# Sigmoid attention and routed rows on one core: scores and values interleaved by halves, routed work in one block a step

## The chip, the core and the metric

The kernel runs on one core of a Trainium2 chip. The metric is the device time of one execution in microseconds (us); lower is better. TensorE (PE) multiplies, VectorE (DVE) and ScalarE (ACT) work element-wise, GpSimd (POOL) and SyncE (SP) here mostly issue DMAs. Each engine works through its own list of instructions in order and waits at semaphores for the others.

## The reference

Two layers in fp32, one behind the other. The first is attention with a sigmoid in place of softmax; the second routes the best 128 tokens of each of the 8 sequences through a small MLP.

```python
# q, k, v: (8, 12, 448, 64)
scores = scale * q @ k^T - log(448)
x = (sigmoid(scores) @ v)            # then as (8, 448, 768)
# w_gate: (768,), w1: (768, 1024), w2: (1024, 768), capacity: 128
scores = einsum('bsd,d->bs', x, w_gate)
out = x.copy()
for b in range(8):
    top = argpartition(-scores[b], 128)[:128]
    xe = x[b, top]
    g = sigmoid(scores[b, top])
    out[b, top] = xe + g[:, None] * (maximum(xe @ w1, 0) @ w2)
```

## The kernel before

**Attention.** The 8 x 12 heads are taken as 24 quads of four heads; a step `s` (12 of them) takes two quads, and three quads make a batch. q and k are loaded token-major (`raw_q`, `raw_k`), turned on DVE in 32x32 blocks (`turn`, two buffers each), and the scores are computed transposed, so that keys lie on partitions. All attention matmuls are 32x64 tiles of weights on 448 columns: sixteen for one *unit* of scores (`unit`, L311; seven units a step), which fill two PSUM tiles `psc` of two heads each; ACT applies the sigmoid to each tile (L319, "squash" below) and puts it into SBUF. Values are computed by `values(s, n)` in four rounds a step (L359), each round accumulating into the two PSUM tiles `o0` (first quad) and `o1` (second). `values(s, 0)` follows unit 6 of its step, and rounds 1 to 3 follow units 0 to 2 of the next step. When the fourth round is done, `take` (L377) transposes each half of `o0` and `o1` on DVE into the batch's activations `x_b`, four takes a step; only then can the two PSUM tiles hold something else. PSUM is full: two `psc`, `o0`, `o1`, two banks each.

**Routing.** For each quad `gate_part` multiplies x_b with the gate weights and sums (L385, L388, two of each a quad). With a batch's third quad `gate` adds up the parts (L403 to L418) and issues a DMA of the 448 scores to DRAM on POOL (L413). `spread` then reads them back as a copy on all 128 partitions, `rep` (L425, POOL's queue too). `ranking` compares every score with the scores that a partition holds (L433, L436) and makes a one-hot matrix `hot` of the ranks (L446, L448; for batches 2 to 5 also two sums of it, L457 and L461). `choose` multiplies it on PE into the 128 chosen tokens (L472, L476), `fetch` turns that into indices and gathers these rows of `out`, which `store` has written.

**Routed work.** Two batches make a pair. Chosen rows are transposed on PE (`turn_rows`, L518). The two products with w1 and w2 are done in seven block products each, after Strassen's scheme: `first` (24 matmul records, L557) and `second` (8, L622), with sums of weight quarters that `make_sum` computes once on DVE, keeps in DRAM and `lend` loads into attention buffers that are free for a while. 28 first and 28 second products are made; the table `WORK` puts most of them behind units 3, 4 and 5 of steps 4 to 11, the rest into `rest()` behind the last step.

**Order.** The schedule is manual: the order of the program is the order of each engine. `gap(s, n)` follows each unit with values, items of `WORK`, gates and what `put` has registered: `spread(b)` after unit 4 of the step in which the batch is complete, `ranking(b)` after unit 1 of the step behind it (for batch 1, after the takes of that step), `choose` some units later in it. In steps 1 to 3, in which there is no routed work yet, `keep_busy` (L332) puts four matmuls of no use between units.

Of the kernel before, what the change touches and what calls it, by code (L numbers as in the profile page):

```python
# [17 lines left out]
def kernel(  # L18
# [11 lines left out]
    nc = tc.nc  # L30
# [31 lines left out]
    raw = ctx.enter_context(tc.tile_pool(name="raw", bufs=2))  # L62
    vals = ctx.enter_context(tc.tile_pool(name="vals", bufs=1))
    head = ctx.enter_context(tc.tile_pool(name="head", bufs=2))
# [6 lines left out]
    ps_sc = ctx.enter_context(tc.tile_pool(name="ps_sc", bufs=2, space=PSUM))  # L71
    ps_o = [ctx.enter_context(tc.tile_pool(name=f"ps_o{n}", bufs=1, space=PSUM))
            for n in range(2)]
    turns = [0, 0]

    def banks(which):
        if which == "any":
            turns[1] ^= 1
            which = "psc" if turns[1] else "o"
        if which == "psc":  # L80
            return ps_sc.tile([P, 2, 512], F32, name="psc")
        if which == "o":
            turns[0] ^= 1
            which = turns[0]
        return ps_o[which].tile([P, 2, 512], F32, name=f"o{which}")


    raws, raw_v = {}, {}

    def load(i):  # L90

        if i >= NQ:
            return
        if i == 2:
            both = moe.tile([P, 6 * KH * P], F32, name="rows_t")
            raws[i] = [both[:, n * TB * Dh:(n + 1) * TB * Dh] for n in range(2)]
        else:
            raws[i] = [raw.tile([P, TB * Dh], F32, name=f"raw_{nm}") for nm in "kq"]
        for t, src in zip(raws[i], (k, q)):
            nc.sync.dma_start(  # L100
                out=t, in_=bass.AP(tensor=src.tensor, offset=src.offset + i * 4 * S * Dh,
                                   ap=[[TB * Dh, P], [1, TB * Dh]]))

    def load_v(s):


        if s >= NS:
            return
        if s in (1, 3):
            tv = [moe.tile([P, D], F32, name="xe", bufs=3).rearrange("p (h c) -> p h c", h=4)  # L110
                  for _ in range(2)]
            at = 2 * QW + s // 2 * 4 * Dh
            th = room["all"][:, at:at + 4 * Dh].rearrange("p (h c) -> p h c", h=4)
        else:
            t = vals.tile([P, 8, NF * Dh], F32, name="raw_v")
            tv = [t[:, :4], t[:, 4:]]
            th = vals.tile([P, 4, Dh], F32, name="raw_h")
        raw_v[s] = (tv, th)

        def blocks(h, r, nh, n):  # L120
            return bass.AP(tensor=v.tensor,
                           offset=v.offset + (8 * s + h) * S * Dh + r * Dh,
                           ap=[[TB * Dh, TT], [S * Dh, nh], [1, n * Dh]])

        for m in range(4):
            rows = slice(m * TT, (m + 1) * TT)
            if s in (1, 3):
                for x in range(2):
                    nc.sync.dma_start(out=tv[x][rows], in_=blocks(4 * x, NF * m, 4, NF))
            else:  # L130
                nc.sync.dma_start(out=t[rows], in_=blocks(0, NF * m, 8, NF))
        for n in range(4):
            nc.sync.dma_start(out=th[n * TT:(n + 1) * TT],
                              in_=blocks(4 * (n // 2), HK + n % 2, 4, 1))


# [4 lines left out]
    assert D == 4 * NF * Dh and 2 * QW + 8 * Dh <= 7 * FH * P  # L141
# [26 lines left out]
    def load_left(m):  # L168

        if m == 1:  # L170
            t = moe.tile([P, 7 * FH * P], F32, name="hidden")
            room["all"], room["a"], room["b"] = t, t[:, :QW], t[:, QW:2 * QW]
        load_quarter(m, room["a"], (1, 0) if m == 1 else (0, 1))

    def make_sum(m, key):
        if (m, key) == (1, 6):
            room["c"] = moe.tile([P, 6 * KH * P], F32, name="rows_t")[:, :QW]
        a, b, c = [room.get(x) for x in "abc"]
        w00, wx, w11 = [(w1_sb, w2_sb)[m - 1][:, x] for x in range(3)]
        dst, x, y, op = {  # L180
            (1, 5): (b, a, w11, ALU.add), (1, 6): (c, b, w00, ALU.subtract),
            (1, 7): (a, w00, a, ALU.subtract), (1, 3): (b, wx, c, ALU.subtract),
            (2, 5): (b, a, w00, ALU.subtract), (2, 6): (c, w11, b, ALU.subtract),
            (2, 7): (a, a, w11, ALU.subtract), (2, 4): (b, wx, c, ALU.subtract)}[m, key]
# [5 lines left out]
    SUMS = {(1, 5): [(1, 5), (1, 6)], (1, 6): [(1, 7), (1, 3)],  # L190
            (2, 5): [(2, 5), (2, 6)], (3, 5): [(2, 7), (2, 4)]}

    def attn_tile(pr, slot):
        return attnp.tile([P, 2, S], F32, name=f"attn{pr}_{slot}")

    def lend(m, key, slot):


        halves = []
        for pr in range(2):  # L200
            if slot == "raw":
                t = raw.tile([P, TB * Dh], F32, name=f"raw_{'kq'[pr]}")[:, :QW // 2]
            elif slot == "turned":
                t = head.tile([P, 2, TB, TT], F32, name=f"{'kq'[pr]}T")
                t = t.rearrange("p e r t -> p (e r t)")[:, :QW // 2]
            else:
                t = attn_tile(pr, slot).rearrange("p a s -> p (a s)")[:, :QW // 2]
            nc.sync.dma_start(out=t, in_=sums[m, key][:, pr * QW // 2:(pr + 1) * QW // 2])
            halves.append(t)
        lent[m, key] = halves  # L210
# [58 lines left out]
    qT, kT, attn, outs = {}, {}, {}, {}  # L269

    def turn(i):


        if i >= NQ:
            return
        kT[i] = head.tile([P, 2, TB, TT], F32, name="kT")
        qT[i] = head.tile([P, 2, TB, TT], F32, name="qT")
        sk, sq = [t.rearrange("p (r e d) -> p e r d", e=2, d=TT) for t in raws.pop(i)]
        for e in range(2):
            nc.vector.transpose(kT[i][:, e, :HK],  # L280
                                sk[:, e, :HK].rearrange("p (m c) d -> p c m d", c=NF))
        nc.vector.transpose(kT[i][:, :, HK:], sk[:, :, HK:])
        if i == 0:
            for e in range(2):
                nc.vector.transpose(qT[i][:, e], sq[:, e])
        else:
            nc.vector.transpose(qT[i], sq)  # L287

    def two_blocks(s):


        return s > 5 and (s, 4) not in WORK

    def unit(s, n):


        if ((s == 0 and n in (1, 3, 5)) or (s in (1, 2, 3) and n == NF + 1)
                or (two_blocks(s) and n == NF + 2)):
            psc = [banks(0), banks(1)]
        else:  # L300
            psc = [banks("psc"), banks("psc")]
        if n == NF:
            parts = [(x, HK) for x in range(2)]
        else:
            x, c = divmod(n, NF + 1)
            parts = [(x, 4 * c), (x, 4 * c + 2)]
        for e in range(2):
            for y, (x, r) in enumerate(parts):
                for h in range(4):
                    d = slice(h * TT, (h + 1) * TT)  # L310
                    nc.tensor.matmul(  # L311
                        psc[h // 2][y * Dh:(y + 1) * Dh, h % 2, :S],
                        kT[2 * s + x][d, e, r:r + 2, :].rearrange("d r t -> d (r t)"),
                        qT[2 * s + x][d, e].rearrange("d r t -> d (r t)"),
                        start=(e == 0), stop=(e == 1))
        for pr in range(2):
            a = attn_tile(pr, f"d{s % 2}{n}" if n < 3 else f"u{n}")
            attn[s, pr, n] = a
            nc.scalar.activation(a, psc[pr][:, :, :S], AF.Sigmoid, bias=bias_s, scale=QK_SCALE)  # L319

    x_tiles, gate_parts, st = {}, {}, {}

    def open_outs(s):
        if s not in outs:
            outs[s] = [banks(0), banks(1)]

    def keep_busy(s):


        open_outs(s)  # L330
        for _ in range(4):
            nc.tensor.matmul(outs[s][0][:, 0, :HP * TT], iden,  # L332
                             wg_b.rearrange("p h t -> p (h t)"), start=True, stop=True)

    def values(s, n):

        tv, th = raw_v[s]  # L340
        if n == 0:
            open_outs(s)
        o = outs[s]
        first = (0, 2, 2, 0)[n]
        quads = [(first + m) % 4 for m in range(4)]
        work = [(r, c) for c in range(NF) for r in quads]
        if n < 2:
            at = 4 * (NF - 1)
            work[at:at] = [(r, None) for r in quads]
        for r, c in work:  # L350
            x, pr = divmod(r ^ n, 2)
            rows = slice(r * TT, (r + 1) * TT)
            for j in range(2):
# [12 lines left out]
        else:  # L366
            for x in range(2):
                for pr in range(2):
                    take(s, pr, x)
# [520 lines left out]
```

## Time and profile before

| what | value |
| --- | --- |
| three runs | 455.09, 455.43, 457.24 us, median 455.43 |
| the profiled execution | 455.12 us, its span 453.3 us |
| PE busy | 441.8 us (97%) |
| DVE, ACT busy | 303.8 us (67%), 180.9 us (40%) |
| mean granted TensorE clock | 0.998 |
| first unit of scores begins | 6.31 us |
| steps 1, 2, 3 (attention alone) | 24.8, 24.7, 25.8 us |
| steps 4 to 11 (with routed work) | 30.4, 35.2, 36.0, 31.8, 36.4, 36.0, 32.5, 30.6 us |
| the rest, behind step 11 | 86.4 us |

The profile records one execution; its span is the time between the first and the last instruction, and the execution's own time is 1.8 us more. Busy time of PE is the time in which a matmul ran, not time at full rate: a matmul that is held up, or records that overlap, count as busy too. Each matmul of fp32 leaves two records. A step is counted from the first record of its values, as a table of windows has it. The chain of waits follows the work that ended last backwards through its releasers.

### The profile page before, as it was taken

Reading aid. Unit: us, or ns where it says so; the run is one execution under the profiler, and the core shown is the slowest. Engines: PE = TensorE matmul, PEld = TensorE weight load, DVE = VectorE, ACT = ScalarE, POOL = GpSimd, SP = SyncE. Lnnn points to the kernel's source line nnn. Section 1 sums busy time; section 2 is a strip of 40 time slices with the busy share of each in tenths; the row PEclk is TensorE's granted clock in tenths of the full one; section 3 lists DMA queues with packets and bytes.
Section 4 is the critical chain, followed back from the end, with each engine's and each line's share of the span. In section 5 each row is a group of like instructions: output and inputs, shape, how many; then the busy total and the mean of one; then the engine's idle time right before and its main releaser. Section 6 shows DMA issues by size and latency. Waiting matters only on the chain.

```text
span 453.3 us, 14449 instructions
## 1 busy us (share of the span) xinstructions
PE 441.8 (97%) x6398; PEld 277.7 (61%) x6398; DVE 303.8 (67%) x663; ACT 180.9 (40%) x234; POOL 32.6 (7%) x55
## 2 busy tenths in 40 slices
PE   8999999999999999999999999999999999999994
PEld 3474745566744845666577854665555648769952
DVE  4308669993854897779633797797662849894472
ACT  3856464555545254335345445324434520101100
POOL 7000000010000000010010000010020001001001
PEclk9999999999999999999999999999999999999999
DMA  8798998999866985985665983995923999711001
GB/s 272 196 342 197 347 345 169 268 196 328 172 208 211 158 228 175 181 193 190 155 235 165 143 219 115 210 176 175 254 80 113 254 212 265 145 36 71 1 0 69
DMA packets 128334, 84.67 MB, mean 187 GB/s; under 512 B 97600, under 2 KB 112064, under 8 KB 128272
## 3 DMA queue, kind: packets, MB, share of 16 engines
q1 hardware_dynamic: 126288, 75.84, 64.9%
q0 software_dynamic: 1984, 7.91, 5.8%
q8 instruction: 50, 0.82, 0.8%
q14 instruction: 12, 0.10, 0.1%
HBM read 63.28 MB, written 20.46 MB: 185 GB/s over the span
## 4 chain that ended last, share of the span: by engine, by line
PE 83%; DVE 9%; DMA 4%; issue 2%; ACT 1%; POOLq 0%; SPq 0%; DVEq 0%
PE o L359 26%; PE psc L311 22%; PE o L557 12%; PE o L622 8%; PE psc L622 5%; PE psc L557 5%; PE o L311 4%; DVE x_b L377 3%; DMA scores<-total 2%; DVE scr L385 1%; DVE gate_p L388 1%; DMA raw_q<-in_q_dram 1%; DVE xe L633 1%; DMA rep<-scores 1%; DMA out_dram<-xe,idx 1%
## 5 line engine op out<-in xcount | busy, mean ns | idle before, releaser
L311 PE MATMUL psc<-qT,kT 32*64 32x448 f32 x2336 | 145.1, 540 | 1.5 <-ACT attn_u L319 0.9
L359 PE MATMUL o<-attn_d,raw_v 32*64 32x448 f32 x960 | 107.6, 535 | 0.1
L359 PE MATMUL o<-attn_u,raw_v 32*64 32x448 f32 x960 | 104.8, 535 | 0.3 <-issue 0.2
L319 ACT ACTIVATE attn_u<-psc,bias_s 128x896 f32<-128x896 f32 x76 | 72.5, 1005 | 76.7 <-PE psc L311 71.3
L311 PEld LDWEIGHTS psc<-qT,kT 32*64 32x64 f32 x2336 | 62.1, 131 | 53.6 <-issue 32.6
L319 ACT ACTIVATE attn_d<-psc,bias_s 128x896 f32<-128x896 f32 x70 | 66.8, 1005 | 46.8 <-PE psc L311 46.7
L377 DVE STREAM_TRANSPOSE x_b<-o 128x448 f32<-128x448 f32 x48 | 26.9, 617 | 63.1 <-PE o L359 55.6
L359 PEld LDWEIGHTS o<-attn_u,raw_v 32*64 32x64 f32 x960 | 44.0, 132 | 21.5 <-issue 17.8
L359 PEld LDWEIGHTS o<-attn_d,raw_v 32*64 32x64 f32 x960 | 43.1, 132 | 17.2 <-issue 14.4
L573 ACT ACTIVATE hidden<-hidden 128x512 f32<-128x512 f32 x12 | 7.5, 630 | 63.2 <-DVE hidden L570 63.2
L557 PEld LDWEIGHTS o<-rows_t,w_sb 128*128 128x128 f32 x264 | 30.3, 192 | 3.8 <-issue 1.4
L557 PE MATMUL o<-rows_t,w_sb 128*128 128x128 f32 x264 | 31.6, 277 | 0.4 <-DVE rows_t L524 0.3
L388 DVE TENSOR_REDUCE gate_p<-scr 128x14 f32<-128x448 f32 x48 | 29.8, 622 | 1.7
L385 DVE TENSOR_TENSOR scr<-x_b,wg_b 128x448 f32<-128x448 f32 x48 | 29.5, 616 | 1.0
L280 DVE STREAM_TRANSPOSE kT<-raw_k 128x384 f32<-128x384 f32 x46 | 23.5, 548 | 7.3 <-DMA raw_k<-in_k_dram 7.3
L433 DVE TENSOR_SCALAR_CACHE_REDUCE scr<-rep,who 128x448 f32<-128x448 f32 (+1 forms) x32 | 21.5, 672 | 9.9 <-DMA rep<-scores 9.1
L557 PEld LDWEIGHTS o<-rows_t,attn_d 128*128 128x128 f32 x216 | 24.7, 192 | 2.6 <-DVE xe L633 1.5
L557 PE MATMUL o<-rows_t,attn_d 128*128 128x128 f32 x216 | 25.7, 276 | 0.6 <-DVE rows_t L530 0.3
L622 PE MATMUL o<-w_sb,hidden 128*128 128x384 f32 x72 | 24.7, 490 | 0.2 <-PE psc L311 0.2
L287 DVE STREAM_TRANSPOSE qT<-raw_q 128x896 f32<-128x896 f32 x22 | 23.6, 1072 | 1.1 <-DMA raw_q<-in_q_dram 1.1
L359 PE MATMUL o<-attn_d,xe 32*64 32x448 f32 x192 | 24.1, 535 | 0.0
L570 DVE TENSOR_TENSOR hidden<-o,hidden 128x512 f32<-128x512 f32 x22 | 14.6, 686 | 13.7 <-PE o L557 13.5
(117 smaller groups left out, 517.9 us busy)
## 6 DMA issues: line engine op xcount, KB each, us to landing
attn_d<-sum SPq DMA_DIRECT2D x42, 384.0 KB, 5.8
out_dram<-x_b SPq DMA_DIRECT2D x32, 336.0 KB, 6.5
raw_k<-in_k_dram SPq DMA_DIRECT2D x23, 448.0 KB
raw_q<-in_q_dram SPq DMA_DIRECT2D x23, 448.0 KB, 6.8
raw_v<-in_v_dram SPq DMA_DIRECT2D x40, 192.0 KB, 8.3
w_sb<-in_moe_w_dram SPq DMA_DIRECT2D x6, 768.0 KB
sum<-hidden SPq DMA_DIRECT2D x6, 768.0 KB, 6.3
rep<-scores POOLq DMA_DIRECT2D x7, 224.0 KB, 5.6
```

The costliest lines, as they stand in the source:

```text
L280: nc.vector.transpose(kT[i][:, e, :HK], sk[:, e, :HK].rearrange("p (m c) d -> p c m d", c=NF))
L287: nc.vector.transpose(qT[i], sq)
L311: nc.tensor.matmul(psc[h // 2][y * Dh:(y + 1) * Dh, h % 2, :S], kT[2 * s + x][d, e, r:r + 2, :].rearrange("d r t -> d (r t)"), qT[2 * s + ...
L319: nc.scalar.activation(a, psc[pr][:, :, :S], AF.Sigmoid, bias=bias_s, scale=QK_SCALE)
L359: nc.tensor.matmul(o[x][j * Dh:(j + 1) * Dh, pr, :S], w, a[rows, j, :], start=(n == 0 and c == 0), stop=(n == 3 and c == NF - 1))
L377: nc.vector.transpose(x_tiles[b][:, :, 2 * g + pr, :], outs[s][x][:, pr, :S].rearrange("p (r t) -> p r t", t=TT))
L385: nc.vector.tensor_tensor(out=tmp, in0=x_tiles[b][:, :, hp, :], in1=wg_b[:, hp:hp + 1, :].to_broadcast([P, TB, TT]), op=ALU.mult)
L388: nc.vector.tensor_reduce(out=gate_parts[b][:, :, hp], in_=tmp, axis=AX.X, op=ALU.add)
L433: nc.vector.tensor_scalar(out=junk[:n], in0=rep[:n], scalar1=own, scalar2=0.0, op0=ALU.is_gt, op1=ALU.add, accum_out=above[:n, c:c + 1])
L557: nc.tensor.matmul(ps[:, f, :n], w((t * FH + f) * P, P), x[:, t, :n], start=(t == 0), stop=(t == KH - 1))
L570: nc.vector.tensor_tensor(out=dst, in0=a, in1=b, op=ALU.add)
L622: nc.tensor.matmul(ps[:n, :DH], h[:, t, :n], w(t * DH, DH), start=(t == 0), stop=(t == FH - 1))
```

## The change

PSUM is held in four tiles that keep their roles: `a1`, `a0` for scores (`PA`), `o1`, `o0` for values (`PO`). The order of one step is that of seven *slots*. A slot is two halves; a half holds four matmuls of scores on two row groups, eight of values on the other two row groups, four of scores again, and one squash. Values run at a distance of four slots: slots 0 to 3 hold rounds 3 to 6 of the step before, slots 4 to 6 rounds 0 to 2 of their own. A unit takes two key blocks of both quads (in `chunks` and `column`; the first four units of step 0 those of one quad). One slot of a step is split, the second part of its values coming ahead of the scores, with a small ACT copy (`join`) between its parts. The takes follow slot 3.

Routed work stands in one `block(s)` after slot 3 of steps 4 to 11, in the order of `BLOCKS`, its products going through the banks of the four tiles from `o0` on. Choices ("c") stand in the blocks too. In `block`, or behind slot 3 where there is none, q and k of the next step are turned; q is turned in place, raw k has one buffer, and the pool of turned q and k has four buffers each. Behind the block come `gates(2s-2)` and `gates(2s-1)`, the gates of both quads of the step before. `spread(b)` comes after slot 5 or 6 of that step, `ranking(b)` after slot 1 of the step behind it, for all batches (the steps of `FULL` are 2, 3, 5, 6, 8, 9, 11 and 12). The sums of the weights are made later (`SUMS`), and lent sums go to buffers of their own (`spares`) after slot 4. `keep_busy` is gone.

The main parts of the diff:

```diff
-    ps_sc = ctx.enter_context(tc.tile_pool(name="ps_sc", bufs=2, space=PSUM))
-    ps_o = [ctx.enter_context(tc.tile_pool(name=f"ps_o{n}", bufs=1, space=PSUM))
-            for n in range(2)]
+    tiles = {}
+    for name in ("a1", "a0", "o1", "o0"):
+        pool = ctx.enter_context(tc.tile_pool(name=f"ps_{name}", bufs=1, space=PSUM))
+        tiles[name] = pool.tile([P, 2, 512], F32, name=name)
+    PA, PO = [[tiles[f"{c}{n}"] for n in range(2)] for c in "ao"]
...
-    SUMS = {(1, 5): [(1, 5), (1, 6)], (1, 6): [(1, 7), (1, 3)],
-            (2, 5): [(2, 5), (2, 6)], (3, 5): [(2, 7), (2, 4)]}
+    SUMS = {(1, 4): [(1, 5)], (1, 6): [(1, 7)], (2, 1): [(1, 6)], (2, 4): [(1, 3)],
+            (4, 4): [(2, 5)], (4, 6): [(2, 7)], (5, 1): [(2, 6)], (5, 2): [(2, 4)]}
...
+            if which == "q":
+                if i:
+                    nc.vector.transpose(heads["q", i], heads["q", i])
...
+    def value(s, half, p, n):
+        for r in (2 * half, 2 * half + 1):
+            x, c, step = chunks(s, n, half)
+            pr = r % 2 ^ p
+            rows = slice(r * TT, (r + 1) * TT)
+            at = column(s, n, half) * Dh
+            i = done[s, x, pr] = done.get((s, x, pr), 0) + 1
+            for j in range(2):
+                nc.tensor.matmul(PO[x][j * Dh:(j + 1) * Dh, pr, :S],
+                                 raw_v[s][rows, 2 * pr + j, at:at + Dh],
+                                 attn[s, pr, n][rows, j, :],
+                                 start=((s, x, pr, j) not in done), stop=(i == TB))
+                done[s, x, pr, j] = True
...
+    BLOCKS = {
+        4: [("t", 0), (1, 0, 1), ("c", 1)],
+        5: [("t", 1), (1, 0, 2), (1, 0, 6)],
+        6: [(1, 0, 7), (1, 0, 4), (1, 0, 5), ("c", 2), (1, 0, 3), (2, 0, 1)],
+        7: [(2, 0, 2), (2, 0, 4), (2, 0, 3), (2, 0, 5), (2, 0, 6), ("c", 3), ("t", 2)],
+        8: [(2, 0, 7), ("t", 3), (1, 1, 1), (1, 1, 2), (1, 1, 6), (1, 1, 7), (1, 1, 4)],
+        9: [(1, 1, 5), (1, 1, 3), (2, 1, 1), ("c", 4), (2, 1, 2), (2, 1, 4)],
+        10: [(2, 1, 3), (2, 1, 5), (2, 1, 6), ("c", 5), (2, 1, 7), ("t", 4)],
+        11: [(1, 2, 1), ("t", 5), (1, 2, 2)],
+    }
...
+    def block(s):
+        places = [("o0", 0), ("o0", 1), ("a1", 0), ("a1", 1), ("a0", 0), ("a0", 1),
+                  ("o1", 0), ("o1", 1)]
+        at = 0
+        for i, item in enumerate(BLOCKS[s]):
...
+            if i == 1:
+                turn("q", 2 * s + 2)
+                turn("k", 2 * s + 3)
+                load("k", 2 * s + 4)
+            if i == 2:
+                turn("q", 2 * s + 3)
...
+    FULL = [(NG * b + NG - 1) // 2 + 1 for b in range(B)]
+    def rounds(s):
...
+        same = [(0, 0, 1), (1, 0, 1), (1, 2, 3), (0, 2, 3), (0, 4, 5)]
+        if s + 1 in BLOCKS:
+            return same + [(1, 4, 5), (1, 0, 6)]
+        return same + [(0, 1, 6), (1, 4, 5)]
...
+    def slot(s, n):
...
+        for half in range(2):
+            pr = 1 - half
+            a, b = entries(vs, i, half)
...
+                score(s, n, 0, pr, PA[pr])
+                value(vs, half, *a)
+                value(vs, half, *b)
+            score(s, n, 1, pr, PA[pr])
...
+            squash(s, n, pr, PA[pr])
+            if i == 6:
+                takes(vs, half)
...
+    def after(s, n):
+        if n == NF and s:
+            if 4 < s:
+                load_v(s)
+            if s in BLOCKS:
+                block(s)
+            else:
+                turn("q", 2 * s + 2)
+                turn("k", 2 * s + 3)
+                load("k", 2 * s + 4)
+                turn("q", 2 * s + 3)
+            gates(2 * s - 2)
+            gates(2 * s - 1)
+        if n == NF + 1:
+            for i, (m, key) in enumerate(LENT.get(s + 1, ())):
+                lend(m, key, i)
...
+        for key in SUMS.get((s, n), ()):
+            make_sum(*key)
...
+        for b in range(B - 1):
+            full = FULL[b]
+            if (s, n) == (full, 5 + b % 2):
+                spread(b)
+            if (s, n) == (full, 6):
+                store(b)
+            if (s, n) == (full + 1, 1):
+                ranking(b)
...
         for s in range(NS):
             for n in range(NU):
-                unit(s, n)
...
+                if n == 0 and s:
+                    load("q", 2 * s + 2, 2 * s + 3)
+                    turn("k", 2 * s + 2)
+                    load("k", 2 * s + 3)
+                slot(s, n)
+                after(s, n)
         rest()
```

## The prediction

> **What bounds the kernel now.** The page comes first: its shares of busy time and the chain that ended last.
>
> ```profile
> PE 441.8 (97%) x6398; PEld 277.7 (61%) x6398; DVE 303.8 (67%) x663; ACT 180.9 (40%) x234; POOL 32.6 (7%) x55
> PE 83%; DVE 9%; DMA 4%; issue 2%; ACT 1%; POOLq 0%; SPq 0%; DVEq 0%
> ```
>
> PE is busy 441.8 of 453.3 us, yet the chain leaves it for 17% of the span. So I ask what PE's records cost at full rate, and what the rest of the chain is. The chain of waits from 57 to 130 us (start, us, what; x counts records, and a matmul is two) answers both:
>
> ```profile
> 59.77 2.24 DVE x_b L377 x4
> ...
> 66.55 7.38 DMA scores<-total
> ...
> 74.50 3.54 DMA rep<-scores
> ...
> 78.07 0.70 DVE scr L433 x2
> ...
> 84.94 1.18 DVE x_b L377 x2
> 86.12 0.14 issue
> 86.26 1.04 PE o L476 x8
> ...
> 98.03 1.50 PE psc L311 x32
> 99.53 3.01 PE o L359 x64
> ```
>
> A unit of scores is 32 records in 1.50 us, two rounds of values 64 in 3.01, so small-tile work costs 0.376 us per 8 records. Further down, the first unit after a 128x128 product takes 1.69, and such a product between units 2.88 where a run of them shows 2.68 each: a change of tile size costs 0.19 each way. Upward is batch 0's routing: quads taken, gates, scores out on POOL at 66.55, copies landed at 78.07, ranking on DVE to 84.9, and then, behind it on the same engine, two takes (L377) for which PE waits.
>
> **Full rate.** The changed kernel has the same products, without keep_busy: 5,376 small records / 32 × 1.504 = 252.7; 28 first products × 2.68 = 75.0; 28 second × 2.58 = 72.2; 8 row turns × 0.66 = 5.3; choosing 5.4. Sum 410.6. With 6.3 us ahead of the first unit (6.31) and 6.0 behind the last matmul (447.3 to 453.3), 422.9. Before, whose span is 453.3, loses 30.4, of which keep_busy is 3 × 1.5.
>
> **Slots.** A slot is one unit of scores plus one round of values, 3.01 us, on other row groups in turn. A score tile's turn is 8 records of scores and 16 of values (3 × 0.376 = 1.13), the last record of its scores (0.53), the squash on ACT (1.00) and some 0.2 of handing over: 2.87, under the 3.01 of a slot, so ACT hides by 0.14. A step is 7 × 3.008 = 21.06; steps 1 to 3 of before took 24.8, 24.7 and 25.8. Losses that stay:
> - Step 0: four units alone need 8 squashes × 0.905 = 7.2 of ACT against 6.0 of PE, and the first squash (1.0) has no cover: 2.2.
> - Split slots of steps 1 to 3 free a score tile late: 3 × 0.5 = 1.5.
> - One block per step: 8 × 0.38, and 0.4 in the rest: 3.4.
> - Block 4's row turn, its copy (0.8) and product wait on each other: 1.0. In blocks 5, 8 and 11 the first item waits for a take of o0 (1.12 with a lag of 0.4, less 0.75 of the other half): 3 × 0.8 = 2.4. After blocks 4, 7 and 10 a bank is drained late: 1.0 in all.
>
> Sum 11.5, so 434.4 us if no routing is waited for.
>
> **Edits at nothing.** Turning q in place is the same instruction (1.07 us), k two of 0.55, sums eight of 1.75 as before; none stands ahead of a take in a step where a ranking does, except the k turn of unit 0 (1.1, under the wait for scores). raw_k has one buffer: its next load is issued after the turn and is wanted three slots (9.0 us) later; q's landing, 6.8, is the nearest row. Were that gap used up, 2 us per step would follow. The lends move behind slot 4 on SP, with eight slots or a block until use. POOL holds only score and copy issues, gathers and scatters, as now.
>
> **The routing chain, the term that decides.** In the changed order on DVE, gates(2s-2) and gates(2s-1) stand behind the block (in steps 2 and 3 behind the turns q, k, q, 3.1 us), and ranking(b) stands at slot 1 of the step after, ahead of the takes of slot 3. DVE works in order. Until the copies of the scores have landed, the ranking waits; the takes wait behind it; and PE's next values or block begin in o0, which those takes free. From the end of the block or slot 3, PE has seven slots, D = 21.06 + 0.2 (b0 21.6; b6 19.2: three slots 9.0, four rounds 6.0, a product 2.7, a choose 1.0, handing over 0.5). In that time must fit: lag δ of DVE; gate parts G, 2.6 a quad (147 to 149.4), one quad for even b, two (5.2) for odd; from L403 to the scores' issue 1.92; L from issue to landed copies; ranking R, 6.95 (78.07 to 85.02), or 9.47 with the added sums (b2 to b5); the first take pair 1.12.
>
> For L, before has 11.5, 11.5, 7.9, 9.4, 10.0, 8.9, 13.5 and 7.6 us: median 9.7. DVE's timeline shows that nothing else is ahead when it waits for this, and that takes come right behind:
>
> ```profile
> 202.92 0.68 DVE L433 TENSOR_SCALAR_CACHE_REDUCE scr<-rep,who 128x448 f32<-128x448 f32 x1 [2.68 <-DMA rep<-scores]
> ...
> 212.37 2.24 DVE L377 STREAM_TRANSPOSE x_b<-o 128x448 f32<-128x448 f32 x4
> ```
>
> Before has steps of 30 to 36 us to hide this; the changed one has 21.3 between blocks. The waits:
> - b0, step 3: 1.4 + 3.1 + 2.6 + 1.9 + 9.7 + 7.0 + 1.1 − 21.6 = 5.2
> - b1, step 4: 1.1 + 3.1 + 5.2 + 1.9 + 9.7 + 7.0 + 1.1 − 21.3 = 7.8
> - b2, step 6: 2.4 + 2.6 + 1.9 + 9.7 + 9.5 + 1.1 − 21.3 = 5.9
> - b3, step 7: 3.1 + 5.2 + 1.9 + 9.7 + 9.5 + 1.1 − 21.3 = 9.2
> - b4, step 9: 1.0 + 2.6 + 1.9 + 9.7 + 9.5 + 1.1 − 21.3 = 4.5
> - b5, step 10: 1.8 + 5.2 + 1.9 + 9.7 + 9.5 + 1.1 − 21.3 = 7.9
> - b6, rest: 1.5 + 2.6 + 1.9 + 9.7 + 7.0 + 1.1 − 19.2 = 4.6
> - b7, whose copies go by SP (7.6): about 1.2.
>
> δ is an estimate from the takes (1.1) or the adds behind a product (0.69 each). Sum 46.3. With L at 7.6 throughout it is 14.7 less, at 11.5 12.6 more.
>
> **The clock.** These would be PE's first long waits, and the trace shows what they bring. Windows after the last matmul (PEclk is the column after the engines), and the launch matmuls, min/median/max in ns:
>
> ```profile
> 447.30:451.40 4.10, 0.00 (x0) 0.00 (x0) 0.62 (x1) 0.00 (x0) 0.97 (x1) 1.00 0.24 96
> 451.40:453.30 1.90, 0.00 (x0) 0.00 (x0) 0.00 (x0) 0.00 (x0) 0.00 (x0) 0.52 0.00 0
> ```
>
> ```profile
> L826 PE MATMUL o<-hot x6: 592/868/1222, 1.5 to 5.1; 128*128 128x512 f32 x6
> ```
>
> After 4.1 us without a matmul the granted clock is 0.52. The launch's first three records come 0.85 to 1.0 apart, the later ones 0.43: a cold start costs 1.3. Seven waits exceed 4.1, five by over 1 us; I take 5 × 1.3 = 6.5, with ends of 0 and 9.1.
>
> The Trainium skill, "TensorE: Matmul & The Clock Gate", Part 1, has the clock at half after an idle window of some 3.4 us, and again full after another such window of work; by that rule a restart would lose about 1.7 us (an estimate), and seven of them 12, which makes the total some 5 us more. The same page, Part 3, says that weight loads overlap matmuls only where the row group differs; that would speak for the halves on differing row groups, but the 0.376 us a wave was reached with same row groups too, so I take no gain from it.
>
> **Sum.** 434.4 + 46.3 + 6.5 = 487.2 us of span. The profiled execution of before took 455.12 for its 453.3, 1.8 more, and the median of its runs is 455.43, 0.3 above that: 489.3 us.
>
> **Rivals.**
> - *The routing is hidden (faster).* If the copies land sooner, in a kernel whose DMA is less crowded, the waits go and 434.4 + 2.1 = 436.5 is left. It decides from L of about 5.7, where waits of 1.2, 3.8, 1.9, 5.2, 0.5 and 3.9 (some 17 us) bring the time to that of before. For it: scores alone have landed in 3.9 at the median. Against: the copies alone took 5.6, and no batch was below 7.6. Chance 0.10.
> - *Halves do not run side by side (slower still).* If the value matmuls of one half, two on the same row group, hold up the scores behind them, each of some 160 halves loses up to 0.75: 120 us; if only a weight load shows (0.05), 8.5. Against: value rounds of before use row groups in several orders, at 3.01 always. Decides when a slot takes over 3.3. Chance 0.05.
> - *The change does less than it says:* slots stay at the pace of ACT, 3.3 to 3.5 us, so steps last longer, the waits shrink by as much, and the loss on the slots of steps without a wait cancels the gain of the block: within 0.5% of before. Chance 0.03.
> - The forecast, waits of 4 to 9 us for b0 to b6: 0.82.
>
> **Range.** L of 7.6 without a clock loss gives 434.4 + 31.6 + 2.1 = 468.1, L of 11.5 with 9.1 gives 504.5; seven estimates of δ, wrong by 0.7 each, add 5 either way: 463 to 509. Half a per cent (2.3 us) is about what runs of this kernel can tell from no change. Faster 0.10, same 0.02, slower 0.88 (the third rival is split over same and slower).
>
> **What would show it.** Right: slots of 3.0 us in steps without a wait; seven PE gaps of 4 to 9 us at L377 takes in steps 3, 4, 6, 7, 9, 10 and the rest, with "rep" as what DVE's L-for-ranking group waited for; PEclk below 1 just behind them. Wrong: copies that land before DVE reaches the ranking, gaps under 2 us, or slots above 3.3.

## The result, and the profile after

The changed kernel takes 546.48 us (median of four runs) against 456.14 for the kernel before on the same chip: a ratio of 1.197, 95% interval 1.189 to 1.205. The forecast was 489.3 us within 463 to 509. The direction was right; the size was more than twice too small, and the time lies outside the range. Here and below, times and ratios leave out executions in a slower state of the chip (three of e4's six, one of e7's four).

The page of the changed kernel: busy time by engine, the granted clock in 40 slices, and the chain that ended last.

```profile
PE 456.9 (84%) x6374; PEld 258.6 (48%) x6374; DVE 305.3 (56%) x643; ACT 188.4 (35%) x225; POOL 33.2 (6%) x55
...
PEclk9999998579899989997999999879978999799998
...
PE 56%; DVE 19%; DMA 10%; issue 7%; SPq 4%; ACT 2%; POOL 0%; POOLq 0%; DVEq 0%; ACTq 0%
```

PE now leads the chain for 56% of 540.9 us instead of 83% of 453.3, and the clock row, all nines before (0.998 on average), has dips. The page and tables of 1 us windows give the loss: PE is idle 84.0 us (540.9 − 456.9; 11.5 before), and the clock is missing for 20.8 us of PE's busy time (0.0 before; the sum of one minus PEclk, times PE's busy share). The two account for 93.3 us, less 4.5 for keep_busy that is gone: 88.8, and the spans differ by 87.6.

**The slots are as forecast.** ACT's timeline, one squash for each half of a slot:

```profile
149.42 1.01 ACT L336 ACTIVATE attn<-a,bias_s 128x896 f32<-128x896 f32 x1 [0.46 <-PE a L322]
150.96 1.01 ACT L336 ACTIVATE attn<-a,bias_s 128x896 f32<-128x896 f32 x1 [0.53 <-PE a L322]
152.45 1.01 ACT L336 ACTIVATE attn<-a,bias_s 128x896 f32<-128x896 f32 x1 [0.49 <-PE a L322]
```

The first and the third, one slot apart, start 3.03 us from each other; ACT waits half a microsecond for PE each time, not PE for ACT. The time is lost elsewhere, in three places. The first is step 3, in the chain of waits:

```profile
80.20 0.70 SPq L389
...
80.94 5.73 SPq L389
...
86.72 2.91 SPq L389
...
89.67 2.68 SPq L389
...
92.45 2.67 SPq L101
...
95.72 4.93 DMA raw_k<-in_k_dram
...
100.67 1.17 DVE kT L304 x2
101.85 0.99 DVE qT L296
...
110.61 0.16 DVE idx L476
110.76 0.08 DVE got L479
...
110.89 1.02 PE o L351 x4
```

SP's queue issues the four stores of batch 0 (L389) for 12 us before it comes to the loads of q and k (L101). DVE cannot turn what has not come; behind the turns stand two quads of gates, and only behind those the two reads (L476, L479) of the tokens chosen for batch 0, which lie in the second bank of o1. PE waits for that bank from 93.36 to 110.89: 17.5 us. And it comes back cold (the number after the engines is the granted clock):

```profile
98.00:110.00 12.00, 0.00 (x0) 0.00 (x0) 9.95 (x21) 0.00 (x0) 0.10 (x1) 0.50 0.79 203
110.90:113.00 2.10, 2.10 (x24) 1.14 (x32) 0.00 (x0) 0.00 (x0) 1.07 (x2) 0.50 0.95 138
```

The second and third are in block 6, again the chain of waits:

```profile
185.28 4.57 DMA rep<-scores
...
189.96 0.70 DVE scr L428 x2
...
199.40 1.18 DVE x_b L372 x2
...
200.62 4.31 PE o L546 x24
...
204.96 1.30 DVE hidden L559 x2
...
206.30 2.96 PE o L546 x24
...
212.03 1.30 DVE hidden L559 x2
...
213.38 0.61 PE a L465 x4
```

This is the wait that the prediction ("the record" in the expectations below) forecast: copies of the scores, ranking, take, then PE's first product, for which PE stood still for 4.15 us. But it then goes on: that product, which begins at half clock (0.67 on average from 200.60 to 205.00), needs 4.31 us instead of 2.68, and the next one waits until DVE has read the first (204.96 to 206.26), and later ones again. The first product is in bank 0 of o0, the second in bank 1 of the same tile. No such wait was in the prediction.

### The profile page after: what moved, and what is told of

The parts are those of the page before. It is cut to its first block, busy times and chain, and to the rows that moved or that the text cites. A ratio compares the mean times of both kernels' runs of the same rounds, so it can differ in the third digit from the quotient of the medians.

```text
span 540.9 us, 14311 instructions
## 1 busy us (share of the span) xinstructions
PE 456.9 (84%) x6374; PEld 258.6 (48%) x6374; DVE 305.3 (56%) x643; ACT 188.4 (35%) x225; POOL 33.2 (6%) x55
## 4 chain that ended last, share of the span: by engine, by line
PE 56%; DVE 19%; DMA 10%; issue 7%; SPq 4%; ACT 2%; POOL 0%; POOLq 0%; DVEq 0%; ACTq 0%
PE a L322 14%; PE o L351 13%; PE o L546 8%; PE o L610 6%; PE a L546 6%; PE a L610 6%; DMA rep<-scores 4%; SPq L389 2%; DMA scores<-total 2%; DVE scr L431 2%; DVE scr L428 2%; ACT attn L336 2%; DVE hidden L559 2%; DVE x_b L372 2%; DVE xe L621 2%
## 5 line engine op out<-in xcount | busy, mean ns | idle before, releaser
L322 PE MATMUL a<-qT,kT 32*64 32x448 f32 x2624 | 256.5, 544 | 7.7 <-ACT attn L336 5.9
L336 ACT ACTIVATE attn<-a,bias_s 128x896 f32<-128x896 f32 x162 | 162.0, 1007 | 146.0 <-PE a L322 93.1
L351 PE MATMUL o<-attn,raw_v 32*64 32x448 f32 x2176 | 206.3, 541 | 0.2 <-issue 0.2
L322 PEld LDWEIGHTS a<-qT,kT 32*64 32x64 f32 x2624 | 92.1, 132 | 105.3 <-ACT attn L336 71.1
L351 PEld LDWEIGHTS o<-attn,raw_v 32*64 32x64 f32 x2176 | 73.6, 132 | 36.8 <-issue 30.2
L351 PE MATMUL o<-attn,rows_t 32*64 32x448 f32 x448 | 45.6, 565 | 19.8 <-DVE got L479 17.5
L304 DVE STREAM_TRANSPOSE kT<-raw_k 128x448 f32<-128x448 f32 x42 | 24.2, 616 | 36.6 <-PE a L322 19.5
L546 PE MATMUL o<-rows_t,spare 128*128 128x128 f32 x192 | 29.4, 323 | 10.3 <-DVE x_b L372 8.1
L546 PEld LDWEIGHTS o<-rows_t,spare 128*128 128x128 f32 x192 | 28.2, 236 | 12.2 <-DVE x_b L372 9.7
L296 DVE STREAM_TRANSPOSE qT<-qT 128x896 f32<-128x896 f32 x23 | 25.2, 1094 | 10.4 <-DMA qT<-in_q_dram 10.4
```

Of the source, the lines that this page charges most:

```text
L296: nc.vector.transpose(heads["q", i], heads["q", i])
L322: nc.tensor.matmul(out[y * Dh:(y + 1) * Dh, h % 2, :S], kt[d, e, r:r + 2].rearrange("d r t -> d (r t)"), qt[d, e], start=(e == 0), stop=(e ...
L336: nc.scalar.activation(a, psc[:, :, :S], AF.Sigmoid, bias=bias_s, scale=QK_SCALE)
L351: nc.tensor.matmul(PO[x][j * Dh:(j + 1) * Dh, pr, :S], raw_v[s][rows, 2 * pr + j, at:at + Dh], attn[s, pr, n][rows, j, :], start=((s, x, p ...
L546: nc.tensor.matmul(ps[:, f, :n], w((t * FH + f) * P, P), x[:, t, :n], start=(t == 0), stop=(t == KH - 1))
```

## Experiments

Times are medians beside the kernel before on the same chip, as a ratio to it; the changed kernel stands at 1.197. The experiments ran on several chips, so a gain is told as the difference of two ratios, times 456 us, and is good to some 5 us; the expectations use plain differences of medians.

**e1: stores behind the loads.** `store(b)` goes from slot 6 of its step to behind the loads of the next (batch 6's to the start of the rest).

```diff
-            if (s, n) == (full, 6):
+            if (s, n) == (full + 1, 0):
                 store(b)
```

> The stores of a batch (four DMA issues on SP) move behind the loads of q and k of the next step. Theory A (SP's queue): the four issues take SP 9.7 to 14.9 us, the loads of step 3 behind them are late, so the turns, the gates and the indices of choose(0) are late, and PE waits 17.5 us in step 3. Without the stores ahead, DVE turns at once and reaches the indices near 101 instead of 110.8: about 10 us less, 535 to 538 against 546.5. Theory B (the record: only takes behind the ranking count, transfers are hidden): no change, 546 within 2.

527.05 us, 1.147 (1.141 to 1.152). Theory A: the loads come early, and PE's wait in step 3 falls from 17.5 to 9.1 us. The gain of 23 is twice what I expected. PE's idle time falls by 13.9 us, 8.4 of them in step 3, and the loss by the clock by 3.7: the waits ahead of blocks 9 and 10 shrink too, from 4.0 to 0.6 and from 7.0 to 5.3, while those ahead of blocks 6 and 7 grow by 1.2 and 0.5. What is left of the wait in step 3 is DVE's own order, turns and gates ahead of the reads.

**e2: batch 0's choice ahead of the turns.** The stores stay; the choice's old place, in slot 4 of step 3, is empty.

```diff
             else:
+                if s == FIRST - 1:
+                    fetch(*choose(0, PO[1][:, 1]))
                 turn("q", 2 * s + 2)
```

> choose(0) and its two reads of the bank stand ahead of the turns and gates of step 3 on DVE instead of behind them; the stores stay. Theory A (order on DVE: PE waits for the reads of the bank o1, which are queued behind three turns and two quads of gates, and these behind late loads): the 17.5 us wait goes, up to 2 us come back as a late turn at step 4; 529 to 533. Theory B (the late loads alone make the wait): the wait only moves to slot 0 of step 4, since its turns are as late as before; 540 to 546.

536.08 us, 1.174 (1.163 to 1.184), a gain of 10, between the theories. The 17.5 us are gone, but 10.5 appear at step 4's takes, ahead of the row turn.

**e6: both.**

> The edits of e1 and e2 together. Theory A (two causes in a row: the late loads by SP's stores, and the indices queued behind turns and gates on DVE): the wait of 9.1 us that e1 left in step 3 and the 10.5 that e2 left in step 4 both go; 527.1 less 9 to 13, so 514 to 518. Theory B (one wait that only moves): no better than e1 alone, 525 to 529.

528.68 us, 1.159 (1.154 to 1.163): 5 us behind e1, so my sum of gains fell. Its chain of waits tells why:

```profile
100.87 7.62 DMA scores<-total
...
109.03 7.09 DMA rep<-scores
...
122.83 1.18 DVE x_b L372 x2
...
124.06 1.56 PE o L507 x6
```

With the wait of step 3 gone, batch 1's copies (15 us here, behind a gather on POOL) and its ranking hold up the takes of step 4: PE stands for 10.9 us. It is the wait that was forecast for b1 (7.8). In the changed kernel it cost nothing: batch 1's scores were issued at 109.9, just before PE's wait of 17.5 us ended, and its ranking was done when PE came to the takes of step 4.

**e3: the ranking behind the takes.**

```diff
-            if (s, n) == (full + 1, 1):
-                ranking(b)
...
         if n == NF and s:
+            for b in range(B - 1):
+                if s == FULL[b] + 1:
+                    ranking(b)
```

> ranking(b) moves from slot 1 of its step to behind the takes of slot 3, ahead of the block and the gates. Theory A (the record: takes behind the ranking hold PE): the PE gaps at the first product of blocks 6, 7, 9 and 10 (4.2, 5.7, 4.0, 7.0 us) and the 2.0 in step 3 go, with about 6 us of half clock behind them; if nothing takes their place, 517 to 523. Theory B (a new wait in place of the old one): now the ranking's 7.0 to 9.5 us stand ahead of the reads of the block's products on DVE, PE waits for these in the second product, and the time stays at 540 to 552.

557.46 us, 1.218 (1.211 to 1.226): 10 us slower, by the mechanism of theory B and beyond its range. The chain in block 6:

```profile
199.71 1.14 DVE x_b L372 x2
200.85 0.58 DVE scr L428 x2
...
209.90 0.35 DVE sums L456
210.25 1.21 DVE hidden L559 x2
...
211.50 5.35 PE o L546 x24
```

The takes are early, but the ranking's 9.5 us now stand between them and the reading of the first product, and the second product (at 211.50) waits for that.

**e4: block items in the four tiles in turn,** bank 0 of each.

```diff
-        places = [("o0", 0), ("o0", 1), ("a1", 0), ("a1", 1), ("a0", 0), ("a0", 1),
-                  ("o1", 0), ("o1", 1)]
+        places = ["o0", "a1", "a0", "o1"]
         for i, item in enumerate(BLOCKS[s]):
+            both = banks(places[i % 4])
```

> Each item of a block takes the next of the four PSUM tiles (o0, a1, a0, o1) instead of the second bank of the same tile. Theory A: a product into the second bank of a tile waits until DVE or ACT have read the first bank, since the wait is on the tile; the gaps inside blocks 5 to 10, 20.7 us in all, mostly go, and 528 to 534 is left. Theory B (the record, which gave nothing for this: only the first item of a block waits): 546 within 2.

509.12 us, 1.108 (1.102 to 1.114): the largest gain of a single edit, 40 us, and more than theory A gave it. In block 6 the second product now follows the first at once, in another tile:

```profile
198.04 5.49 PE o L546 x24
203.53 2.81 PE a L546 x24
```

The gaps inside blocks 5 to 10 fall from 20.7 to some 6 us, most of it at the ends of blocks 6 and 9; the rest of the gain is not divided further.

**e5: the order of a split slot.**

```diff
+            value(vs, 0, one, u); join(0); score(s, n, 0, 1, PA[1])
+            value(vs, 1, one, u); join(1); score(s, n, 0, 0, PA[0])
+            score(s, n, 1, 1, PA[1]); squash(s, n, 1, PA[1])
+            for half in range(2): value(vs, half, two, u)    # and the takes
+            score(s, n, 1, 0, PA[0]); squash(s, n, 0, PA[0])
```

> Only the order within a split slot is changed: values of both quads come first and the second part of the scores for a1 ahead of the second part of the values, so that each score tile has about 1.1 us more between its squash and its next use. Theory A (a score tile is freed too late; two PE gaps of 0.47 us in each of eleven split slots of 3.9 us): split slots fall to 3.1 or 3.2, 546.5 becomes 537 to 540. Theory B (the two parts of the values wait for the small ACT copy between them): the gaps stay and so does the time, 546 within 2.

544.12 us, 1.190 (1.186 to 1.195): not to be told from 1.197 (1.189 to 1.205); the difference is 3 us. Split slots fell from 3.9 to 3.6 or 3.7 us only; inconclusive as to what holds the rest.

**e9: matmuls of no use in the waits.** 40 in step 3 and 9 to 16 ahead of blocks 6, 7, 9 and 10, each fill meant to be shorter than its wait.

```diff
                 fetch(*choose(0, PO[1][:, 1]))
+                fill(PA[0], 40)
...
             if s in BLOCKS:
+                fill(PA[1], {6: 9, 7: 13, 9: 9, 10: 16}.get(s, 0))
                 block(s)
```

> The changed kernel with matmuls of no use put into its waits, as keep_busy did: 40 in step 3 (15 us for a wait of 17.5), 9, 13, 9 and 16 ahead of blocks 6, 7, 9 and 10 (3.4 to 6 us for waits of 4.0 to 7.0), each a little shorter than the wait, so that nothing is delayed. They compute nothing that is used. Theory A (half clock behind each wait is a cost of its own, 20.8 us in the trace where the record took 6.5): the first product of a block falls from 4.3 to 5.5 us back to 2.6 to 2.7, and 546.5 becomes 532 to 538. Theory B (the clock recovers within the time that the waits take anyway, or the waits grow by as much): 545 to 549.

534.69 us, 1.170 (1.162 to 1.179): work that nobody uses makes the kernel 12 us faster. The chain in block 7, the fill (L668) and the first products behind it:

```profile
243.00 4.49 PE a L668 x26
247.49 2.59 PE o L610 x8
...
250.78 2.86 PE o L610 x8
```

2.59 us where the changed kernel had 5.50, although in blocks 7, 9 and 10 the fill ran 0.2 to 0.6 us past the take. So half clock behind a wait is a cost beside the wait.

**e7: e1, e2, e4 and e5 together.**

> e1, e2, e4 and e5 together, the routing chain left as it is (gates behind the block, ranking ahead of the takes). By the sum of the single gains (19, 10, 33 and 8 us) it is 476 to 480; what should be left in the profile are the takes behind the ranking at blocks 6, 7, 9, 10 and in the rest, about 20 us of gaps with some 6 of half clock. If these were only the shadow of the other waits, 450 to 460.

494.59 us, 1.089 (1.080 to 1.098), a gain of 49 where the four single ones (23, 10, 40 and 3) sum to 76: the waits cover one another. Of the 27 that are missing, 16 are those of e1 and e2, as e6 showed (17 instead of 33). In its block 6 the take still waits for the ranking and the first product is cold, but products run back to back:

```profile
187.42 1.18 DVE x_b L372 x2
...
188.65 5.49 PE o L546 x24
194.14 5.45 PE a L546 x48
...
199.93 2.80 PE o L546 x24
```

**e8 and e10: the routing moved.** In e8 the rankings of batches 1 to 5 stand behind takes and block, the choices in slot 1 of the step after that, through a0; batch 0's gates stand ahead of the turns; batch 6's ranking is in the rest. The items of a block take the tiles in another order, and the copies for odd batches are issued later, in slot 1 of the next step.

```diff
             block(s)
+            for b in range(1, B - 1):
+                if s == FULL[b] + 1:
+                    ranking(b)
             gates(2 * s - 2)
             gates(2 * s - 1)
...
+            if n == 1 and half == 0:
+                for c in range(1, B - 2):
+                    if s == FULL[c] + 2:
+                        fetch(*choose(c, PA[0][:, 0]))
```

> e7 with the routing chain moved out of the takes' way: for batches 1 to 5 the ranking stands behind the takes and behind the block, ahead of the gates, and the choice in slot 1 of the step after that, through the free score tile a0; batch 0's gates stand ahead of the turns; batch 6's ranking stands in the rest behind the first products' sums; block items take tiles so that the last two are in a0 and o1. Theory A (the record's: the takes behind the ranking cost waits and clock): all PE gaps over 1.5 us go, PEclk stays at 1; full rate 422.9 plus 2 for step 0, 4 for the slots of steps 0 and 1, 3.4 and 5 for changes of tile size (six more choices between slots), about 5 for the rest, 2 outside the span: 442 to 450, faster than the kernel before. Theory B (DVE itself is short of time in a 21 us step with ranking, gates and turns): waits of the same size appear at the turns or the sums, 465 to 480.

495.48 us, 1.089 (1.083 to 1.095): no gain on e7, and worse than both theories. The waits at the blocks went, and others came behind the choices. DVE's timeline and PE's show it:

```profile
207.18 0.69 DVE L413 COPY who<-by_token 32x4 f32<-32x4 f32 x4
207.88 1.17 DVE L304 STREAM_TRANSPOSE kT<-raw_k 128x448 f32<-128x448 f32 x2
208.97 0.12 DVE L477 TENSOR_SCALAR idx<-a 128x1 int32<-128x1 f32 x1
```

```profile
201.97 0.61 PE L466 MATMUL a<-ones,sums 128*128 128x1 f32 x4
209.21 1.02 PE L322 MATMUL a<-qT,kT 32*64 32x448 f32 x4 [6.63 <-DVE got L480]
```

A read of 0.12 us stands on DVE behind gates and a turn, and PE's scores in the same tile wait 6.6 us for it. e10 puts these gates behind the choice, and in the rest the choices of batches 6 and 7 later:

```diff
+        if n == 1 and s - 2 in FULL[1:]:
+            gates(2 * s - 4)
+            gates(2 * s - 3)
```

> e8 with the gates of the steps that rank moved behind the choice of the next step (so that the two reads of the chosen tokens no longer queue behind 10 us of gates on DVE), and in the rest the choices of batches 6 and 7 one and two products later. Theory A (e8's waits of 1.9, 6.6, 3.7, 6.2 and 2.1 us at the scores behind a choice, and 1.7 and 4.3 in the rest, are DVE's order alone): all go, with about 6 of half clock; 495.5 becomes 460 to 468. Theory B (DVE has no room: the same time appears at the takes, the turns or the next ranking): 480 to 495.

472.9 us, 1.035 (1.028 to 1.042), a gain of 25 on e8, between the theories. Of the waits behind the choices one of 1.1 us is left, and the others are 0.4 each. The time is 5 us above what I expected, since a wait of 7.0 us in the rest, at the second products behind batch 7's ranking, came in place of two shorter ones (1.7 and 4.3).

**e11: the rest and batch 0's choice.** The diff shows the choice and the gates behind it; the order in the rest changes too, as the expectation says.

```diff
+            if (s, n, half) == (FIRST - 1, NU - 1, 0):
+                fetch(*choose(0, PA[0][:, 0]))
...
+        if (s, n) == (FIRST - 1, NU - 1):
+            gates(2 * s - 2)
+            gates(2 * s - 1)
```

> e10 with batch 0's choice in slot 6 of step 3 (it waited 1.4 us for the ranking and stood ahead of the turns), the gates of that step behind it, the gates that complete batch 6 ahead of block 11, its ranking at the start of the rest, and two sums ahead of batch 7's ranking. Theory A: DVE gets 7 us earlier through the rest, so the 7.0 us wait at the second products goes with some 2 of half clock, and 3.5 in step 3: 472.9 becomes 459 to 463, level with the kernel before or up to 1.5% slower. Theory B (the rest is bound by DVE's own work, about 45 us against PE's 36): 466 to 473.

473.22 us, 1.036 (1.034 to 1.039): the same as e10, so theory A fell, and as much was lost as won. The 7.0 us in the rest became 3.7 at the choice, and 5.9 came up in step 5:

```profile
113.00 7.91 SPq L389
...
120.96 2.65 SPq L389
...
123.65 3.02 SPq L389
...
126.77 7.32 DMA raw_k<-in_k_dram
...
134.75 0.60 DVE kT L304
...
135.52 1.02 PE a L322 x4
```

The stores of batch 1 are on SP again when a load of k is wanted, and raw k has a single buffer; its turn stands ahead of the choice's read on DVE.

**e12: e11 with the stores back ahead of the loads.**

```diff
-            if (s, n) == (full + 1, 0):
+            if (s, n) == (full, 6):
                 store(b)
```

> e11 with one part undone: the stores stand again where the change put them, behind slot 6 and so ahead of the next step's loads of q and k on SP. Theory A (SP's 10 to 15 us of store issues delay the loads, and the loads the turns): in steps 3, 4, 6, 7, 9 and 10 the loads come 10 us later, are turned behind slot 3 and delay what DVE does behind them, 8 to 20 us more than e11. Theory B (the loads have slots to spare once DVE's order is mended, and the earlier stores let the gathers start earlier): within 2 us of e11, or less.

479.01 us, 1.050 (1.047 to 1.053), 6 us more than e11, between the theories: the wait in step 5 shrinks to 1.8, but one of 8.0 comes in step 3. Stores and loads of k on one queue cost several microseconds in either order; no run put the stores on another queue.

## Why the prediction was wrong, step by step

The mechanism of the prediction was one of several, and the sum failed in the terms that it did not have: the wait of 17.5 us in step 3, the waits inside the blocks, and most of the clock.

- **Slots** (3.01 us, ACT hidden): right, 3.0 in nearly all unsplit slots from step 2 on. Those of steps 0 and 1 took 3.2 to 4.0, up to about 4 us over eight slots that the prediction lacked.
- **Split slots** (1.5 in three steps): wrong in number. Eleven slots of 3.9 instead of 3.0, 10 us, of which 6 are PE gaps of 0.4 to 0.5 (two in a slot in steps 1 to 3, one in steps 5 to 11). e5 recovered a third of it at best.
- **Takes behind the ranking** (46.3): right in kind and place, too large. The gaps are 2.0 (b0), none (b1), 4.2, 5.7, 4.0, 7.0 and 2.4, 25 us in all. The forecasts from b2 to b6 were 5.9, 9.2, 4.5, 7.9 and 4.6: each is 0.5 to 3.5 too long. The copies were not the error: they took 8.4 to 10.9 us for b0 to b6, against 9.7. For b3, the longest, DVE was 0.6 us behind PE at the end of the block, where δ was taken as 3.1. b1's was covered, as e2 and e6 show. Nor can the wait be had back by one edit: moving the ranking behind the takes alone (e3) costs 10 us.
- **"Edits at nothing"** failed. I looked at lends, turns and sums, but did not follow `store` past the loads on SP, though the kernel before puts the stores of batches 0 and 1 at several places between loads. I took 6.8 us of landing for q and k and not the issues queued ahead of them. And I did not ask where the reads of `choose(0)` stand on DVE. Together: the 17.5 us wait; e1 alone is worth 23 us, e2 10.
- **Blocks** ("the first item waits for a take"): wrong, the largest term. Two products in the halves of one tile are separated by DVE's or ACT's reading of the first: 20.7 us of gaps, 40 us by e4. Before alternates tiles, so its trace had no such row; `places` in the diff had it. The Trainium skill, "PSUM — Partial Sum Buffer", "Summary: rules for kernel authors", says that PSUM is to be read beside a running matmul in a different bank. e4 does this across tiles. Within a tile of two banks it is the program that waits for the whole tile: in the chain of block 6 the product into bank 1 begins when DVE has read bank 0. e4 shows the cost of the wait; a kernel that waits per bank was not run.
- **The clock** (6.5, with ends of 0 and 9.1): 20.8 us in the trace. About 12 of them lie around the five waits that e9 fills, and e9 gained 12. About 9 lie elsewhere: inside block 9 behind a wait of 5.1 us, behind 2.3 us in block 10 and 2.4 in the rest, and at 142.1 in step 4, where the clock is 0.50 for 3.4 us although no wait in the 8 us before was longer than 0.95. Too few waits were in the sum, and 1.3 us for each, from the launch, was too little: the first products behind the waits in blocks 6, 7, 9 and 10 alone take 1.6 to 2.9 us longer. The Trainium skill, "TensorE: Matmul & The Clock Gate", Part 1, gives some 1.7 a restart by the prediction's estimate; that is nearer, and still too little here.
- **434.4 us without waits** was too low. Busy time above the full-rate 410.6, clock taken out, is 25.5 us in the changed kernel (540.9 − 84.0 − 20.8 − 410.6) and 26.7 before (453.3 − 11.5 − 4.5 − 410.6). In e10 it is 468.9 − 26.4 − 3.6 − 410.6 = 28.3. So most of the loss that the interleaving was counted to remove is still there; the prediction had 30.4 fall to 11.5. By lines of the trace, more than half of it is in the attention records: 267.2 us of busy time at full clock in the changed kernel against 252.7 at full rate, and 270.8 before. The slots that stand free of waits and blocks do run in 3.0; the excess is in the first two steps (4.5) and in split slots and those beside a wait or a block (10). The products take 152.3 against 147.2, and the launch matmuls 4.8.

The extra gaps add up: 25 at the takes, 17.5 in step 3, 20.7 inside blocks 5 to 10, 6 in split slots, and 5 in block 4 and in short waits at the ends of other blocks are 74 us, against 72.5 more idle time than before, which had some gaps of its own.

Of the rivals, none was right: the waits at the takes are in the trace, and the halves run side by side. Whether a version on these slots can beat the kernel before stays open. The best that ran, e10 and e11, is 3.5% slower, with nearly the same busy time above full rate and 14 to 15 us more idle time.

## What to carry over

Ahead of a reordering, list for every wait on a tile not only who reads it, but everything that stands ahead of that reader on its engine, and everything ahead of the loads on the issuing queue: short reads (0.12 us here) queued behind ten microseconds of other work cost as much as the work. Price waits with their restart, and do not add up the gains of several mended waits: on one path they cover each other. Two products that follow each other belong in different PSUM tiles where the program waits per tile.

## What the runs showed of the hardware

- Stores of 336 KB each, four in a row, keep SP's queue issuing for 9.7 to 14.9 us in the changed kernel (9.0 to 9.7 before, where four stand together), and the loads behind them wait.
- After a wait of 4 to 17 us the granted clock is 0.50, and a 128x128 product that comes next (behind 4 to 7 us) takes 4.3 to 5.5 us instead of 2.6 to 2.7; in e9, filling four such waits with other matmuls brought the next product back to 2.6 to 3.0.
- The clock also fell to 0.50 without such a wait: from 142.1 to 145.4 in the changed kernel, behind a row turn, a product and a choice with waits of 0.4 to 0.95 us between them. PE was busy for 2.2 of the 3.4 us before.
